# Load order, one more dependence of the planner, and the last stage's sums in two halves: a kernel of a spectral filter and a token MLP

## The chip, the cores and the metric

The kernel runs on one core of a Trainium2 chip. A core has five engines that run side by side and wait for each other by semaphores: TensorE (PE in the profile; its weight loads are PEld) multiplies matrices, VectorE (DVE) and ScalarE (ACT) work element by element, GpSimd (POOL) is nearly unused here, and SyncE (SP) issues the transfers (DMAs). Data lie in SBUF, with 128 partitions; TensorE writes to PSUM, which is handed out in banks. The metric is the device time of one execution in microseconds.

## The reference

Two results are mixed by a gate. Cut to what matters, with x of shape 2048 x 512 (S x D):

```
g = sigmoid((x * gate_w).sum(-1))                    # one number per row of x
a = irfft2(rfft2(x) * (w_r + i w_i))                 # spectral filter, in f32, then bf16
h = layernorm(x)                                      # over D, without weights
u = gelu(einsum("sd,sf->df", h, w1) + b1)            # mixes rows: 2048 -> 1792
b = (einsum("df,fs->ds", u, w2) + b2).T              # 1792 -> 2048
out = g * a + (1 - g) * b
```

Both branches are given the same x, the input A_x; the input B_x is not used. Inputs and output are bf16.

## The kernel before, in words

The 2048 rows are dealt out as 16 blocks j = 4q + r of 128 rows: q is the quarter, r the residue of the row's number modulo 4. A row block is one [128, 512] slice of the tile `x`; the four blocks of one r form a row group.

The work has these stages. (1) Loads of x, group by group, with the transform tables (`ta`, one part per r) and the first-layer weights in between (`w1`, buffer `wa`, first seven column tiles of 128). (2) For each row block VectorE (L487, L488) or ScalarE (L491, L495) takes mean and variance, and ScalarE (L527) or VectorE (L521) writes the normalized h. (3) TensorE multiplies h with w1 (`m1`, L705), seven column tiles side by side in seven PSUM banks, then seven more with the weights in `wb`; ScalarE applies the gelu (L721). (4) Beside it runs the spectral branch: sums over quarters (`q4a`, `q4b`, L535 to L542), a transform over rows on TensorE (`fa`, L554 to L557), copied out by ScalarE (L560), sums (`d2`, L566 and L567), a radix-4 step (`radix4`, L585 to L601), a transform over columns (`fb`, L653, with table `tb`; copied out by L660), sums (`tb2`, L669 to L677), the product with the filter (L820 to L846), and the way back: the inverse radix-4 step, whose two parts of results for each half lt are called ("T", lt, 0) and ("T", lt, 1), the inverse transform over rows (`i1`, L886 to L898, for each r, each half lt and each h) and the sums behind it (L914 to L927). (5) The gate: x times `gate_w` (tile `gw`, L730, VectorE, four times [128, 2048]), summed by ScalarE (L735), then g and 1 - g. This overwrites x, so each multiply has to wait until its group was read by all others. (6) The second layer (`m2`, L1008) for each row block, evacuated by ScalarE with the factor 1 - g (L1014). (7) The last stage, for eight pairs of row blocks p: TensorE transforms over columns (`i3`, L967 to L970), ScalarE copies out with the factor g (L974), VectorE makes the sums of the pair (`es`, L982 to L993: a short copy, an add and a sub into the tile `es`, then an add and a sub out of it), adds the MLP's part (`fin2`, L1027) and SP stores. The last block is finished in parts by L1021.

The order of all this is made by a planner when the kernel is built (class `Plan`, L133). Each task has an engine, a duration, what it reads and writes, a priority (a small number goes first) and, where it uses one of a few buffers, the buffer's name in `alloc` and `free`. The planner simulates all engines with these durations and, whenever an engine is free, takes the ready task of the smallest priority; between tasks of equal priority the one that was added first. A task on the same VectorE is ready only 0.1 us after the task that it depends on ended; in that moment any other ready task is taken. Loads are tasks of SP: nearly all are ready from the start, so SP issues them in the order of their priorities, one at a time, and a load may be issued only when the eighth before it has landed. The resulting order is fixed for each engine; on the chip an engine executes its own list in this order and waits wherever an input is late.

The code names of the loads: `ld([("x", r, q) ...])` x of group r, `ld([("ta", r)])` the row table of group r, `ld_w1` the first weights of group r (for r = 1 in two halves of q), `load_wb(0)` four wide pieces of w1 for `wb`, 512 KB each, `load("gw")` the gate row copied to all partitions, `load("tb")` the column table, `b2h` the second bias, and `ld_W` the complex filter weights.

Of the kernel before, what the change touches and what calls it, by code (L numbers as in the profile page):

```python
# [16 lines left out]
P = 128  # L17
S = 2048
D = 512
# [113 lines left out]
class Plan:  # L133
# [11 lines left out]
    def add(self, eng, dur, emit, reads=(), writes=(), prio=0.0, alloc=(), free=(), nbytes=0, after=(), late=0.0):  # L145
        t = Task()
        t.late = late
        t.eng, t.dur, t.emit, t.prio = eng, dur, emit, prio
        t.alloc, t.free, t.nbytes = tuple(alloc), tuple(free), nbytes
        t.users, t.end, t.ready = [], None, 0.0  # L150
        deps = set(after)
        for k in reads:
            if k in self.last_w:
                deps.add(self.last_w[k])
            self.readers.setdefault(k, []).append(t)
        for k in writes:
            if k in self.last_w:
                deps.add(self.last_w[k])
            deps.update(self.readers.get(k, ()))
            self.last_w[k] = t  # L160
            self.readers[k] = []
        deps.discard(t)
        t.deps = deps
        self.tasks.append(t)
        return t
# [99 lines left out]
def kernel(  # L265
# [22 lines left out]

    pool = ctx.enter_context(tc.tile_pool(name="sb", bufs=1))
    psum = ctx.enter_context(tc.tile_pool(name="ps", bufs=1, space=bass.MemoryType.PSUM))  # L290
    NES = 1

    def sb(shape, dt, tag, bufs=1):
        return pool.tile(shape, dt, tag=tag, name=tag, bufs=bufs)
# [48 lines left out]
    def load(key, shape, dt, src, nbytes, prio=0.0):  # L343
        def emit():
            t[key] = sb(shape, dt, key)
            dma(t[key][:], src)
        return add("SP", 0.5, emit, writes=[key], prio=prio, nbytes=nbytes)

    def ld(keys, dst, src, nbytes, prio, eng="SP"):
        return add(eng, 0.5, lambda: dma(dst(), src, A if eng == "ACT" else None), writes=keys, prio=prio, nbytes=nbytes, after=[a0])  # L350
# [21 lines left out]
    for r in range(4):  # L372
        if r == 0:
            for n, qs in enumerate(XQ):
                ld([("x", 0, q) for q in qs], lambda qs=qs: t["x"][:, qs[0]:qs[-1] + 1:2, 0, :], x4[:, qs[0]:qs[-1] + 1:2, 0, :], 131072 * len(qs), -9 + 0.1 * n)
        else:
            for qs in ((0,), (1,), (2, 3)) if r == 1 else ((0, 1, 2, 3),):
                c = slice(qs[0], qs[-1] + 1)
                ld([("x", r, q) for q in qs], lambda r=r, c=c: t["x"][:, c, r, :], x4[:, c, r, :], 131072 * len(qs), 2 * r - (3 if r == 1 else 0) + 0.01 * qs[0])
        ld([("ta", r)], lambda r=r: t["ta"][:, r, :], tabs["ta"][:, r, :], 163840, 2 * r + (0.6 if r == 1 else 0.2) if r else -0.8)  # L380

    NF = 7
    WB = (0, NF, NF + 4, NFT)
# [23 lines left out]
    def ld_bias():  # L407
        dma(t["b1b"][0:NFT], B_b1.rearrange("(t f) -> t f", f=P))
    add("SP", 0.5, ld_bias, writes=["bias"], prio=7.1, nbytes=4096, after=[a0])
    load("tb", [P, 776], BF16, tabs["tb"], 198656, prio=9)  # L410

    def ld_wb(k, q):
        def emit():
# [10 lines left out]
            add("SP", 0.5, ld_wb(k, q), writes=[("w1", k + 1, 4 * q + r) for r in range(4)], prio=10 + 12 * k + 0.1 * q,  # L424
                nbytes=131072 * (WB[k + 2] - WB[k + 1]), after=after)
    load_wb(0)
    load("gw", [P, D], BF16, gate_w[None, :].to_broadcast([P, D]), 131072, prio=14.5)

    ld(["b2h"], lambda: t["b2h"][:], B_b2.rearrange("(q p r) -> p q r", q=4, r=4), 300000, 14.6)

    wsrc = (A_w_r, A_w_i)

# [440 lines left out]
    for rs, h in ((0, 0), (0, 1), (1, 0), (1, 1)):  # L873
        for r in (rs, rs + 2):
            for lt in range(2):
                tag = ("fa", "fb")[lt]

                def i1(h=h, r=r, lt=lt, tag=tag):
                    if "zz" not in t:
                        t["zz"] = sb([P, 2, 2, 2, 2, 2, 2, P], BF16, "X")  # L880
                        t["ze"] = sb([P, 2, 2, 2, 2, L], BF16, "h")
                    p1 = t["i1", h, r, lt] = ps([P, 2, L], F32, tag, 2)
                    o, w = ti_at(r)
                    ti = t["ti"][:, o:o + w]
                    for v in range(2):
                        d = lambda c: t["B"][:, lt, r, 2 * c + v, h:L:2]  # L886
                        if r % 2:
                            for c in range(2):
                                f = (2 * c if lt == 0 else 5 - c) * P
                                T.matmul(p1[:, v], lhsT=d(c), rhs=ti[:, f:f + L], start=(c == 0), stop=(c == 1))  # L890
                        else:
                            n = 129 if r == 0 and lt == 0 else P
                            u = ti[:, 256 * lt:256 * lt + 256]
                            if n > P:
                                T.matmul(p1[:, v], lhsT=d(1), rhs=t["ti"][:, 2816:3072], start=True, stop=False)
                            else:
                                T.matmul(p1[:, v, n:], lhsT=d(1), rhs=u[:, n:], start=True, stop=True)
                            T.matmul(p1[:, v, 0:n], lhsT=d(0), rhs=u[:, 0:n], start=(n == P), stop=True)  # L898
                i1t[h, r, lt] = add("PE", mm(*([256] * 4 if r % 2 else [128] * 4)), i1, reads=[("T", lt, r % 2), "ti"], writes=[("i1", h, r, lt)], prio=3, alloc=[tag])

                def i1ev(h=h, r=r, lt=lt):
                    if r % 2:
                        o = t["zz"][:, 1, h, lt, :, :, r // 2, :]
                        A.copy(o, t["i1", h, r, lt][:].rearrange("p v (k a) -> p v k a", k=2))
                    else:
                        A.copy(t["ze"][:, h, r // 2, lt], t["i1", h, r, lt][:])
                add("ACT", act(512), i1ev, reads=[("i1", h, r, lt)] + pbk, writes=[("zz" if r % 2 else "ze", h, r, lt)], prio=1.7, free=[tag], after=[lined])

            if r % 2 == 0:
                def zf(h=h, r=r):  # L910
                    e = t["ze"][:, h, r // 2]
                    k0, k1 = (t["zz"][:, 0, h, :, :, k, r // 2, :] for k in range(2))
                    if r == 0:
                        V.tensor_copy(k0[:, :, :, 0], e[:, :, :, 0])  # L914
                        V.tensor_copy(k1[:, :, :, 0], e[:, :, :, P])
                        V.tensor_add(k0[:, :, :, 1:P], e[:, :, :, 1:P], e[:, :, :, P + 1:L])
                        V.tensor_sub(k1[:, :, :, P - 1:0:-1], e[:, :, :, 1:P], e[:, :, :, P + 1:L])
                    else:
                        V.tensor_add(k0, e[:, :, :, 0:P], e[:, :, :, P:L])
                        V.tensor_sub(k1[:, :, :, ::-1], e[:, :, :, 0:P], e[:, :, :, P:L])  # L920
                add("DVE", 2 * tt(512) + (tiny(2) if r == 0 else 0), zf, reads=[("ze", h, r, lt) for lt in range(2)], writes=[("zz", h, r, lt) for lt in range(2)], prio=3.55)

        def fq(rs=rs, h=h):
            z = xph(h)[:, 2048 * rs:2048 * rs + 2048].rearrange("p (q v n) -> p q v n", q=4, v=2)
            a, b = (t["zz"][:, rs, h, i].rearrange("p v k r a -> p k v (r a)") for i in range(2))
            V.tensor_add(z[:, 0:4:3], a, b)
            V.tensor_sub(z[:, 1:3], a[:, ::-1], b[:, ::-1])  # L927
        add("DVE", 2 * tt(1024), fq, reads=[("zz", h, r, lt) for r in (rs, rs + 2) for lt in range(2)] + [("T", 0, 0), ("T", 0, 1), ("T", 1, 0), ("T", 1, 1)],
            writes=[("z", rs, h)] + ([] if rs else ["pp" if h else "xs"]), prio=3.6)
# [27 lines left out]
    for p in range(NJ // 2):  # L957
# [22 lines left out]
            return t["tb_"][:, j0:j0 + 3:2]  # L980

        def es(p=p, j0=j0, late=late, tb2j=tb2j):  # L982
            e, s = eo_v(p), sb([P, 2, 2, 2, P], BF16, "es", NES)
            o = tb2j() if late else e
            if late:
                for i in range(2):
                    V.tensor_scalar_add(e[:, i, 0, 0:129], e[:, i, 0, 0:129], t["ombb2"][:, j0 + 2 * i:j0 + 2 * i + 1])
            o = o.rearrange("p j h (k d) -> p j (h k) d", k=2)
            V.tensor_copy(s[:, :, :, :, 0], e[:, :, :, 0:129:128].rearrange("p j h k -> p j k h"))
            V.tensor_add(s[:, :, 0, :, 1:P], e[:, :, :, 1:P], e[:, :, :, P + 1:L])  # L990
            V.tensor_sub(s[:, :, 1, :, P - 1:0:-1], e[:, :, :, 1:P], e[:, :, :, P + 1:L])
            V.tensor_add(o[:, :, 0:4:3], s[:, :, :, 0], s[:, :, :, 1])
            V.tensor_sub(o[:, :, 2:0:-1], s[:, :, :, 0], s[:, :, :, 1])  # L993
        add("DVE", tiny(1) + 4 * tt(512) + (0.3 if late else 0), es, reads=(k1 + ["omg"]) if late else [],
            writes=ko if late else k1, prio=4, alloc=["es"], free=["es"], after=gates if late else ())

        for i, j in enumerate((j0, j1)):
            n = 2 * p + i
# [77 lines left out]
```

## Time and profile before

| | us |
|---|---|
| median of 3 runs (lowest, highest) | 129.49 (129.37, 129.72) |
| the profiled execution | 129.0 |
| its span, first to last instruction | 127.1 |
| TensorE busy | 122.3 |
| VectorE busy | 114.6 |
| ScalarE busy | 81.3 |

The profile is of one execution. A row of a timeline gives start, duration, engine, line of the kernel, operation, what is written <- what is read with its shape, and how many instructions were merged (x7); in brackets stands how long the engine had been idle and what ended it. A row of the wait view gives who waited <- for whom: total, how many times, the longest. A row of the view by stretches gives the stretch, its length, the busy time of PE, PEld, DVE, ACT and POOL with their numbers of instructions, the granted TensorE clock (1.00 is full), the mean busy share of the 16 DMA engines and GB/s. The line that begins with GB/s gives the rate in 40 equal slices of the span, 3.18 us each. The granted clock was 1.00 over the whole span.

### The profile page before, as it was taken

The page shows a single profiled execution, that of the slowest core. Times are in us where ns is not written, and L with a number is a line of the kernel's source. Part 1 is how long each engine was busy: PE and PEld are TensorE (multiplying, and loading weights), DVE is VectorE, ACT ScalarE, POOL GpSimd, SP SyncE. Part 2 cuts the span into 40 slices and gives each one's busy share as a digit, 9 for nine tenths or more (in the row PEclk, how much of TensorE's full clock was granted, in tenths as well). Part 3 has the DMA queues.
Part 4 walks back from the last instruction along what each step waited for, and adds up shares of the span by engine and source line. Part 5 has one row for each costly group of instructions (what it writes and reads, how often), then busy time and mean ns, then how long its engine had stood idle before and what let it go on. Part 6 is the DMA issues. An engine that isn't in the chain of part 4 may idle for free.

```text
span 127.1 us, 2153 instructions
## 1 busy us (share of the span) xinstructions
PE 122.3 (96%) x756; PEld 68.9 (54%) x756; DVE 114.6 (90%) x273; ACT 81.3 (64%) x165; POOL 0.2 (0%) x4
## 2 busy tenths in 40 slices
PE   6999999999999999999999999999989999999991
PEld 2345555555555466644445555555667767655590
DVE  2789999996999999999999999999989989999951
ACT  0973789699999999999420004722389999952200
POOL 0000000000000000000000000000000000000000
PEclk9999999999999999999999999999999999999999
DMA  2999999995548946899999900000000000006451
GB/s 69 300 355 291 382 366 368 351 325 106 122 107 256 285 96 143 200 406 415 411 409 406 398 29 0 0 5 0 3 0 0 0 5 0 0 0 248 165 211 44
DMA packets 18219, 23.12 MB, mean 182 GB/s; under 512 B 2190, under 2 KB 15904, under 8 KB 18208
## 3 DMA queue, kind: packets, MB, share of 16 engines
q1 hardware_dynamic: 17616, 22.36, 52.8%
q10 hardware_dynamic: 592, 0.62, 1.6%
q8 instruction: 6, 0.10, 0.3%
q14 instruction: 5, 0.04, 0.1%
HBM read 20.86 MB, written 2.10 MB: 181 GB/s over the span
## 4 chain that ended last, share of the span: by engine, by line
DVE 37%; PE 29%; DMA 21%; SPq 8%; issue 2%; DVEq 0%
PE acc L1008 16%; DMA wa<-in_B_w_dram 12%; SPq L306 8%; DMA gw<-in_gate_w_dram 6%; DVE x L730 4%; DVE xp L828 4%; DVE st L828 3%; DMA x<-in_A_x_dram 3%; DVE st L586 3%; PE acc L705 3%; DVE xp L833 2%; DVE xp L585 2%; DVE B L840 2%; DVE xp L834 2%; PE fb L890 1%
## 5 line engine op out<-in xcount | busy, mean ns | idle before, releaser
L705 PE MATMUL acc<-h,wb 128*128 128x512 bf16 x112 | 26.9, 379 | 0.0
L1008 PE MATMUL acc<-gl,wb 128*128 128x512 bf16 (+1 forms) x98 | 24.6, 371 | 0.0
L1008 PE MATMUL acc<-gl,wa 128*128 128x512 bf16 (+1 forms) x98 | 23.8, 371 | 0.0
L1014 ACT ACTIVATE x<-acc,ombb,omg 128x512 bf16<-128x512 f32 x12 | 9.0, 777 | 21.4 <-PE acc L1008 21.4
L1008 PEld LDWEIGHTS <-wa 128*128 128x128 bf16 x126 | 13.5, 113 | 9.9
L1008 PEld LDWEIGHTS <-wb 128*128 128x128 bf16 x126 | 13.3, 113 | 9.3
L705 PE MATMUL acc<-h,wa 128*128 128x512 bf16 x64 | 17.6, 379 | 0.0
L705 PEld LDWEIGHTS <-wb 128*128 128x128 bf16 x112 | 10.7, 98 | 10.5
L705 PEld LDWEIGHTS <-wa 128*128 128x128 bf16 x112 | 10.3, 98 | 10.4 <-issue 0.8
L487 DVE BATCH_NORM_STATS2 stats<-x 128x6 f32<-128x512 bf16 x14 | 9.5, 678 | 1.9 <-DMA x<-in_A_x_dram 1.9
L560 ACT CAST xp<-fa 128x512 bf16<-128x512 f32 x16 | 9.2, 580 | 2.0 <-PE fa L557 2.0
L735 ACT ACTIVATE x<-x 128x512 bf16<-128x512 bf16 x16 | 10.2, 692 | 0.0
L721 ACT ACTIVATE gl<-acc,b1f 128x512 bf16<-128x512 f32 x11 | 7.9, 719 | 3.5 <-PE acc L705 3.5
L705 PE MATMUL fb<-h,wa 128*128 128x512 bf16 x32 | 9.7, 379 | 0.0
L527 ACT ACTIVATE h<-x,nmr,rstd 128x512 bf16<-128x512 bf16 x11 | 8.4, 807 | 1.1 <-DVE nmr L518 1.1
L705 PE MATMUL fa<-h,wa 128*128 128x512 bf16 x16 | 5.9, 381 | 0.1
L653 PEld LDWEIGHTS <-X 128*128 128x128 bf16 x64 | 4.6, 98 | 2.5 <-DVE X L637 0.7
L974 ACT ACTIVATE B<-fa,g 128x512 bf16<-128x512 f32 x8 | 5.6, 704 | 0.2 <-PE fa L970 0.2
L730 DVE TENSOR_TENSOR x<-x,gw 128x2048 bf16<-128x2048 bf16 x4 | 4.8, 1220 | 1.1 <-DMA gw<-in_gate_w_dram 1.1
L974 ACT ACTIVATE B<-fb,g 128x512 bf16<-128x512 f32 x8 | 5.7, 712 | 0.0
L356 PE MATMUL fa<-xp 128*128 128x512 bf16 x10 | 4.4, 632 | 1.2 <-DVE xp L317 1.2
L660 ACT CAST X<-fb 128x512 bf16<-128x512 f32 x8 | 5.1, 636 | 0.0
(169 smaller groups left out, 232.8 us busy)
## 6 DMA issues: line engine op xcount, KB each, us to landing
wb<-in_B_w_dram SPq DMA_DIRECT2D x11, 512.0 KB
wa<-in_B_w_dram SPq DMA_DIRECT2D x7, 512.0 KB
wa<-in_B_w_dram SPq DMA_DIRECT2D x2, 896.0 KB
wb<-in_B_w_dram SPq DMA_DIRECT2D x4, 384.0 KB
out_dram<-x SPq DMA_DIRECT2D x3, 512.0 KB
x<-in_A_x_dram SPq DMA_DIRECT2D x2, 512.0 KB
wa<-in_B_w_dram SPq DMA_DIRECT2D x2, 448.0 KB
rot<-dft_ti SPq DMA_DIRECT2D x1, 768.0 KB
```

The lines of the kernel that those rows point to most:

```text
L306: (eng or nc.sync).dma_start(out=out_ap, in_=in_ap)
L487: V.bn_stats(out=t["stats"][:, j, :], in_=t["x"][:, j // 4, j % 4, :])
L527: add("ACT", 0.71, lambda j=j: A.activation(t["h"][:, j // 4, j % 4, :], t["x"][:, j // 4, j % 4, :], ActF.Identity, bias=t["nmr"][:, j:j ...
L560: add("ACT", act(512), lambda r=r, dq=dq: A.copy(xe(r)[:, :, :, dq, :], t["pa", r, dq][:]), reads=[("pa", r, dq)], writes=[("X", r, dq)], ...
L705: T.matmul(t["u", ft][:], lhsT=w[:, j // 4, j % 4, c * P:(c + 1) * P], rhs=t["h"][:, j // 4, j % 4, :], start=(j == jorder[0]), stop=(j == ...
L721: gelus.append(add("ACT", act(512, 1) , lambda ft=ft: A.activation(t["gl"][:, ft, :], t["u", ft][:], ActF.Gelu_apprx_tanh, bias=t["b1f"][: ...
L730: add("DVE", tt(2048), lambda r=r: V.tensor_mul(t["x"][:, :, r, :], t["x"][:, :, r, :], t["gw"][:, None, :].to_broadcast([P, 4, D])), read ...
L735: A.activation(t["x"][:, q, r, :], t["x"][:, q, r, :], ActF.Copy, accum_out=t["glog"][:, 4 * q + r:4 * q + r + 1])
L828: V.tensor_mul(o, xs, w)
L974: A.activation(eo_v(p)[:, n], t["i3", j][:], ActF.Copy, scale=t["g"][:, j:j + 1])
L1008: T.matmul(t["y", j, m][:, cs], lhsT=w[:, o, 512 * q + r:512 * q + 512:4], rhs=t["gl"][:, ft, cs], start=(ft == 0), stop=(ft == NFT - 1))
L1014: A.activation(tbuf(j).rearrange("p h d -> p (h d)"), t["y", j, 0][:], ActF.Identity, bias=t["ombb2"][:, j:j + 1], scale=t["omg"][:, j:j + 1])
```

## The change

Four things are changed; the instructions that compute are the same, their order is not.

1. The priorities of loads. Issued before, behind the first x and weights: w1 of r = 1 (two halves), ta 1, x 2, ta 2, w1 of r = 2, x 3, ta 3, w1 of r = 3, flip, b1, tb, four wide pieces, gw, b2h. Issued after: w1 of r = 1 (first half), x 2, ta 1, w1 of r = 1 (second half), w1 of r = 2, x 3, ta 2, w1 of r = 3, flip, b1, gw, ta 3, four wide pieces, tb, b2h.
2. In the planner, the inverse transform `i1` of r = 2 is given a dependence on ("T", lt, 1) beside ("T", lt, 0).
3. The sums of the last stage are split into two tasks, `es` (into the tile `es`) and `es2` (out of it). With equal priorities, the planner may take the first half of the next pair between them.
4. The tile `es` has two buffers instead of one.

```diff
-    NES = 1
+    NES = 2
...
-                ld([("x", r, q) for q in qs], lambda r=r, c=c: t["x"][:, c, r, :], x4[:, c, r, :], 131072 * len(qs), 2 * r - (3 if r == 1 else 0) + 0.01 * qs[0])
-        ld([("ta", r)], lambda r=r: t["ta"][:, r, :], tabs["ta"][:, r, :], 163840, 2 * r + (0.6 if r == 1 else 0.2) if r else -0.8)
+                ld([("x", r, q) for q in qs], lambda r=r, c=c: t["x"][:, c, r, :], x4[:, c, r, :], 131072 * len(qs), (0, -0.9 if len(qs) > 1 else -1 + 0.01 * qs[0], 2.503, 4.6)[r])
+        ld([("ta", r)], lambda r=r: t["ta"][:, r, :], tabs["ta"][:, r, :], 163840, (-0.8, 2.505, 6.3, 7.3)[r])
...
-    load("tb", [P, 776], BF16, tabs["tb"], 198656, prio=9)
+    load("tb", [P, 776], BF16, tabs["tb"], 198656, prio=14.7)
...
-    load("gw", [P, D], BF16, gate_w[None, :].to_broadcast([P, D]), 131072, prio=14.5)
+    load("gw", [P, D], BF16, gate_w[None, :].to_broadcast([P, D]), 131072, prio=7.2)
-    ld(["b2h"], lambda: t["b2h"][:], B_b2.rearrange("(q p r) -> p q r", q=4, r=4), 300000, 14.6)
+    ld(["b2h"], lambda: t["b2h"][:], B_b2.rearrange("(q p r) -> p q r", q=4, r=4), 300000, 14.9)
...
-                i1t[h, r, lt] = add("PE", ..., i1, reads=[("T", lt, r % 2), "ti"], ...)
+                i1t[h, r, lt] = add("PE", ..., i1, reads=[("T", lt, r % 2), "ti"] + ([("T", lt, 1)] if r == 2 else []), ...)
...
         def es(p=p, j0=j0, late=late, tb2j=tb2j):
-            e, s = eo_v(p), sb([P, 2, 2, 2, P], BF16, "es", NES)
+            e = eo_v(p)
+            s = t["es", p] = sb([P, 2, 2, 2, P], BF16, "es", NES)
...
             V.tensor_sub(s[:, :, 1, :, P - 1:0:-1], e[:, :, :, 1:P], e[:, :, :, P + 1:L])
+        add("DVE", 0.08 + 2 * tt(512) + (0.45 if late else 0), es, reads=k1 + (["omg"] if late else []), writes=[("es", p)], prio=4, alloc=["es"],
+            after=gates if late else ())
+
+        def es2(p=p, late=late, tb2j=tb2j):
+            s, o = t["es", p], (tb2j() if late else eo_v(p)).rearrange("p j h (k d) -> p j (h k) d", k=2)
             V.tensor_add(o[:, :, 0:4:3], s[:, :, :, 0], s[:, :, :, 1])
             V.tensor_sub(o[:, :, 2:0:-1], s[:, :, :, 0], s[:, :, :, 1])
-        add("DVE", tiny(1) + 4 * tt(512) + (0.3 if late else 0), es, reads=(k1 + ["omg"]) if late else [],
-            writes=ko if late else k1, prio=4, alloc=["es"], free=["es"], after=gates if late else ())
+        add("DVE", 0.01 + 2 * tt(512), es2, reads=[("es", p)] + k1, writes=ko if late else k1, prio=4, free=["es"])
```

More of the change, by code (lines that the diff above doesn't have):

```diff
@@ L898, in i1 @@
                             T.matmul(p1[:, v, 0:n], lhsT=d(0), rhs=u[:, 0:n], start=(n == P), stop=True)
-                i1t[h, r, lt] = add("PE", mm(*([256] * 4 if r % 2 else [128] * 4)), i1, reads=[("T", lt, r % 2), "ti"], writes=[("i1", h, r, lt)], prio=3, alloc=[tag])
+                i1t[h, r, lt] = add("PE", mm(*([256] * 4 if r % 2 else [128] * 4)), i1, reads=[("T", lt, r % 2), "ti"] + ([("T", lt, 1)] if r == 2 else []), writes=[("i1", h, r, lt)], prio=3, alloc=[tag])
                 def i1ev(h=h, r=r, lt=lt):
@@ L982, in es @@
         def es(p=p, j0=j0, late=late, tb2j=tb2j):
-            e, s = eo_v(p), sb([P, 2, 2, 2, P], BF16, "es", NES)
-            o = tb2j() if late else e
+            e = eo_v(p)
+            s = t["es", p] = sb([P, 2, 2, 2, P], BF16, "es", NES)
             if late:
@@ L987, in es @@
                     V.tensor_scalar_add(e[:, i, 0, 0:129], e[:, i, 0, 0:129], t["ombb2"][:, j0 + 2 * i:j0 + 2 * i + 1])
-            o = o.rearrange("p j h (k d) -> p j (h k) d", k=2)
             V.tensor_copy(s[:, :, :, :, 0], e[:, :, :, 0:129:128].rearrange("p j h k -> p j k h"))
```

## The prediction

> **What bounds the kernel now.** I read the page first, then the timeline of TensorE for holes, then who waits for whom, then the chain that ended last, and then the two other engines where a hole of TensorE begins.
>
> ```profile
> span 127.1 us, 2153 instructions
> PE 122.3 (96%) x756; PEld 68.9 (54%) x756; DVE 114.6 (90%) x273; ACT 81.3 (64%) x165; POOL 0.2 (0%) x4
> ```
>
> TensorE (PE) is busy for 96% of the span, VectorE (DVE) for 90%. Ends of matmuls are modelled, so I don't use the busy time but the distance from start to start:
>
> ```profile
> 32.38 0.22 PE L556 MATMUL fa<-rot,gl 128*128 128x128 bf16 x1
> 32.69 0.23 PE L557 MATMUL fa<-rot,gl 128*128 128x128 bf16 x1
> ...
> 39.37 5.56 PE L705 MATMUL acc<-h,wb 128*128 128x512 bf16 x25
> 45.09 0.40 PE L653 MATMUL fa<-tb,X 128*128 128x128 bf16 x4 [0.16 <-DVE X L637]
> ...
> 93.00 0.22 PE L898 MATMUL fb<-rot,B 128*128 128x128 bf16 x1
> 93.61 0.23 PE L897 MATMUL fb<-rot,B 128*128 128x128 bf16 x1 [0.39 <-DVE B L601]
> ...
> 111.96 1.67 PE L1008 MATMUL acc<-gl,wa 128*128 128x512 bf16 x7
> 113.47 1.67 PE L1008 MATMUL acc<-gl,wb 128*128 128x512 bf16 x7
> ```
>
> Seven 512-column matmuls take 113.47 - 111.96 = 1.51 us, 0.216 us each. A 128-column one takes a quarter, about 0.056. With these pitches three real holes stand in the rows: 32.69 - 32.38 - 0.056 = 0.25 us; 45.09 - (39.37 + 25 x 0.216) = 0.33 us; 93.61 - 93.00 - 0.056 = 0.55 us. Together 1.13 us. In the rows of the wait view all three are waits for VectorE:
>
> ```profile
> PEld L557 <- DVE gl L542: 0.2, 1, 0.2
> PEld L653 <- DVE X L637: 0.7, 1, 0.7
> PEld L897 <- DVE B L601: 0.6, 1, 0.6
> DVE x L730 <- DMA gw<-in_gate_w_dram: 1.1, 1, 1.1
> ```
>
> After 93.6 us there is no hole:
>
> ```profile
> 93.60:124.30 30.70, 30.67 (x240) 21.01 (x240) 26.90 (x72) 20.24 (x36) 0.00 (x0) 1.00 0.18 67
> ```
>
> That is length, then busy time of PE, weight loads, DVE, ACT and POOL, the granted clock (1.00) and the DMA columns. TensorE is the bound, its matmuls are not changed by the edit, and time can only come from holes, or be lost by making new ones.
>
> **The change part by part.**
>
> *The gate row (`gw`) ahead of the wide weights.* Before, it is issued after four 512 KB pieces:
>
> ```profile
> 16.36 6.32 SPq L306 DMA_DIRECT2D wb<-in_B_w_dram  x4
> ```
> ```profile
> 23.07 7.65 DMA gw<-in_gate_w_dram
> ```
>
> It lands 7.65 us after its issue, at 30.72, and VectorE's first multiply by it waits:
>
> ```profile
> 25.43 0.39 DVE L566 TENSOR_TENSOR X<-xp 128x512 bf16<-128x512 bf16 x1
> ...
> 30.74 1.23 DVE L730 TENSOR_TENSOR x<-x,gw 128x2048 bf16<-128x2048 bf16 x1 [1.09 <-DMA gw<-in_gate_w_dram]
> 31.88 0.42 DVE L541 TENSOR_TENSOR gl<-st 128x512 bf16<-128x512 bf16 x1
> 32.22 0.42 DVE L542 TENSOR_TENSOR gl<-st 128x512 bf16<-128x512 bf16 x1
> 32.55 2.35 DVE L730 TENSOR_TENSOR x<-x,gw 128x2048 bf16<-128x2048 bf16 x2
> ...
> 44.78 0.25 DVE L637 CAST X<-fx 128x32 bf16<-128x32 f32 x1
> ...
> 52.66 0.69 DVE L669 TENSOR_TENSOR B<-X 128x1024 bf16<-128x1024 bf16 x1
> ...
> 92.87 0.69 DVE L601 TENSOR_TENSOR B<-st 128x1024 bf16<-128x1024 bf16 x1
> ```
>
> After, the row is issued before the four pieces, so it lands before them, by the four issues at least 6.3 us sooner, some 5 us ahead of the multiply. The 1.09 us go. L542 then ends 1.09 earlier (31.5 instead of 32.6), before TensorE asks for it at 32.44: hole 1, 0.25 us, closes. L637 ends at 43.9; TensorE, itself 0.25 earlier, asks at 44.5: hole 2, 0.33, closes too. TensorE is then 0.58 ahead.
>
> What is late next on VectorE is ScalarE (ACT):
>
> ```profile
> 32.96 0.58 ACT L560 CAST xp<-fa 128x512 bf16<-128x512 f32 x1 [0.21 <-PE fa L557]
> 49.03 0.69 ACT L721 ACTIVATE gl<-acc,b1f 128x512 bf16<-128x512 f32 x1 [0.27 <-PE acc L705]
> 51.98 0.65 ACT L660 CAST X<-fb 128x512 bf16<-128x512 f32 x1
> ```
>
> L669 starts at 52.66, 0.03 us after that copy ends (52.63). ScalarE gains only what it waits for TensorE ahead of this, 0.21 + 0.27 = 0.48 us. So of VectorE's 1.09 about 0.5 is left at 52.7, and as no wait of it stands between there and L601, L601 ends at 93.1 instead of 93.6. Bounds for what is left: 0 (if ScalarE is held by something else) and 1.09.
>
> *The wait that the planner now counts.* A row group r = 2 of the inverse transform is now planned after both parts of the sums it reads (`("T", lt, 1)` too), as the chip already makes it wait: the stalled L897 in hole 3 waits for L601. With hole 3 alone unmended TensorE would come to it 0.58 earlier and VectorE 0.5 earlier, and a wait of about 0.6 would stay. With the new dependence the planner puts other matmuls there: the second layer's (L1008), 0.216 us each, three cover 0.65. They are taken from the closed stretch behind, so hole 3, 0.55 us, comes off the end. Cost: the r = 2 products go out up to 0.65 later; what reads them is ScalarE and VectorE in the last stage, whose cover is below. I take 0.55; the ends are 0 (planner finds no filler) and 0.55 + 0.08.
>
> *The other loads.* x of row group 2 goes ahead of half of the r = 1 weights, x of group 3 ahead of two tables, `tb` behind the wide weights, the tables for 2 and 3 later. No statistic but the very first waits for x, and what is moved back has time:
>
> ```profile
> DVE stats L487 <- DMA x<-in_A_x_dram: 1.9, 1, 1.9
> ```
> ```profile
> 16.88 0.38 PE L705 MATMUL fa<-h,wa 128*128 128x512 bf16 x1
> ```
> ```profile
> GB/s 69 300 355 291 382 366 368 351 325 106 122 107 256 285 96 143 200 406 415 411 409 406 398 29 0 0 5 0 3 0 0 0 5 0 0 0 248 165 211 44
> ```
>
> The moved half is behind 3.74 MB in all (itself in it). By the slices of 3.18 us, 0.22 + 0.95 + 1.13 + 0.93 = 3.23 MB are there at 12.7 and the rest at 14.0; if the next piece (0.92 MB) shares the engines, at 16.4. Its first matmul is at 16.88. So 0, with a cover of 0.5 us or more; if that is gone TensorE pays the difference, at most 0.5. `tb` takes the old place of `gw` behind the wide weights, from where a load landed at 30.72, and is read at 45.09; the last table stands ahead of the wide weights, so it lands before that too, and is read at 32.38. The number of DMAs in front of the complex weights is the same, so SP and what queues behind it (their issues, then the second layer's weights) don't move: 0. The small `b1` row keeps its neighbours: 0.
>
> *The last stage in two halves, and the second tile.* Per row pair the same five VectorE instructions; no instruction is added.
>
> ```profile
> 102.67 0.42 DVE L990 TENSOR_TENSOR es<-B 128x508 bf16<-128x508 bf16 x1
> 103.01 0.42 DVE L991 TENSOR_TENSOR es<-B 128x508 bf16<-128x508 bf16 x1
> 103.54 0.43 DVE L992 TENSOR_TENSOR B<-es 128x512 bf16<-128x512 bf16 x1
> ...
> 106.22 0.42 DVE L993 TENSOR_TENSOR B<-es 128x512 bf16<-128x512 bf16 x1
> 106.74 0.19 DVE L989 COPY es<-B 128x8 bf16<-128x8 bf16 x1
> ...
> 120.15 0.68 DVE L1027 TENSOR_TENSOR x<-x,B 128x1024 bf16<-128x1024 bf16 x1
> 121.23 0.75 DVE L1021 SCALAR_TENSOR_TENSOR x<-acc,omg,x 128x512 bf16<-128x512 f32 x1 [0.39 <-PE acc L1008]
> ```
>
> Two sums that don't depend on each other start 0.34 us apart (102.67, 103.01); the second half starts 0.53 after the first: 0.19 lost. A new pair behind the second half starts 0.52 later, 0.18 lost: the one tile is still in use. With the halves alternating and two tiles, eight times the first and three times the second can go: up to 8 x 0.19 + 3 x 0.18 = 2.1 us of VectorE, at least 0. It is off the path: the last sum ends at 120.83 and VectorE then waits 0.39 for TensorE. If TensorE is 1.13 earlier (120.1 instead of 121.23) and VectorE only 0.5 (120.3), VectorE would be 0.2 late for one row block and catch up in the next wait; any third of the 2.1 us covers it. Priced at 0.
>
> *Sum.* 0.25 + 0.33 + 0.55 = 1.13; I take 1.1. The profiled execution took 129.0 for its span of 127.1, so 127.9 after; it is 0.5 below the median of the runs, 129.49, so the median goes to **128.4 us**.
>
> **The rivals.**
>
> *B, only VectorE's half comes through.* The planner finds no useful filler for hole 3, and the wait of 0.6 stays. Then the end moves with L601, by 0.5: 129.0. For it: the planner's times are not the chip's; hole 3 itself shows that. Against: fillers are there in plenty, the L1008 matmuls that now run in closed rows behind 110 us.
>
> *C and D, the multiplies are pulled forward.* With `gw` early, the planner may place the four L730 (1.14 us each from start to start: 30.74 to 31.88) where it sees VectorE free, ahead of the statistics of group 3. Those have no slack:
>
> ```profile
> 27.14 1.52 ACT L527 ACTIVATE h<-x,nmr,rstd 128x512 bf16<-128x512 bf16 x2 [0.23 <-DVE nmr L518]
> ```
> ```profile
> 28.91 0.38 PE L705 MATMUL fa<-h,wa 128*128 128x512 bf16 x1
> ```
>
> ScalarE finishes the last h at 28.66 and TensorE takes it at 28.91, 0.25 later. One multiply ahead costs 1.14 - 0.25 = 0.89 there and leaves the gain of 1.13: about 129.3, no change (C). Two cost 2.28 - 0.25 = 2.03: slower from the second on, 129.49 - 1.13 + 2.03 = 130.4 (D). Against: they have the lowest priority of what VectorE has, and the sums of group 0 (`d2`, L566, which need only ScalarE's copies of that group) were held back for the statistics until 25.43 in the rows above; any free moment of the plan would have gone to them first. That no other small wait of a newly made plan eats the gain is not shown; I count that with C and D.
>
> *E, VectorE is the bound in the last stage.* If TensorE's closed rows are only the model of their ends, VectorE (26.90 of 30.70 busy) sets the end, and the 0.5 and 2.1 us come off: 126.9. Against: the pitch of 0.216 is between starts, not ends, and VectorE waits 0.39 for TensorE before L1021, not the other way.
>
> The Trainium skill ("Perfetto Trace Analysis", section "Identifying the Most-Contended Engine") calls matmul busy time a bad measure and would judge by weight loads, 54% here, so that VectorE with 90% is the engine to relieve: that is rival E, 126.9. Against E speaks another of its pages, "VectorE: DVE Perf Modes", section "The DRAIN you can't avoid": there a semaphore after each of eight chained copies cost nothing, so that splitting the sums would bring VectorE nothing and only 0.5 of E's time is left, 129.0. The rows above disagree with that second rule, 0.53 against 0.34 us.
>
> **How the numbers follow.** Forecast (A, own range 128.1 to 128.8) 0.48, B 0.13, C 0.15, D 0.20, E 0.04. About 0.3%, 0.39 us, is what a measurement of this kernel can tell from no change. A, B and E are faster by more: 0.65; C is within: 0.15; D is slower: 0.20. The range goes from 128.0 (all of 1.13 and the uncertainty of the runs) up to 130.0, over A, B, C and a part of D; E and most of D are left out.
>
> **What would show it.** In the profile after: no wait of L730 for `gw`; L637 done before 44.2; L669 right behind L660, both about 0.5 earlier; no hole of TensorE at L653 and L897, with L1008 rows between the r = 0 and r = 2 products; first halves of two pairs next to each other on VectorE, with starts of L992 0.34 after what is before it; TensorE's last matmul at about 123.2 instead of 124.3. Wrong it is if an L730 stands ahead of a group 3 statistic (L487), if TensorE waits for ScalarE's h (L527) or for the moved weights at 16.9, or if VectorE is later than TensorE at L1021 by more than 0.8.

## The result, and the profile after

The changed kernel takes 127.74 us (median of 5 runs, 127.68 to 128.14) against 129.37 us for the kernel before in the same comparison (5 runs, 128.64 to 129.72). The ratio is 0.990, with a 95% interval from 0.9866 to 0.9933: 1.3 us faster, 0.9 to 1.7 (the two medians lie 1.6 apart). Four of all the executions told of here, three of the kernel before and the profiled one of the split alone (130.87 us, whose trace is therefore not read), took over 1.5% longer than the shortest of their kernel and are left out of every ratio and range. The profiled executions are 129.0 and 127.68 us, their spans 127.1 and 125.9.

The page of the kernel after:

```profile
span 125.9 us, 2138 instructions
PE 120.5 (96%) x743; PEld 68.8 (55%) x756; DVE 113.8 (90%) x273; ACT 81.0 (64%) x165; POOL 0.2 (0%) x4
```

Thirteen records of matmuls are missing in this trace (743 of 756), each of which looks like a hole of 0.2 us in the timeline; they are no waits, and the weight loads are complete. In its wait view there is no wait of L730 for `gw`, and none of TensorE for L542, L637 or L601. VectorE around `gw`, where the code asks for it, and where ScalarE limits it (timeline of the kernel after; L1024 to L1030 are the old L1021 to L1027, L1011 the old L1008):

```profile
25.42 0.39 DVE L566 TENSOR_TENSOR X<-xp 128x512 bf16<-128x512 bf16 x1
...
29.55 1.22 DVE L730 TENSOR_TENSOR x<-x,gw 128x2048 bf16<-128x2048 bf16 x1
30.69 0.42 DVE L541 TENSOR_TENSOR gl<-st 128x512 bf16<-128x512 bf16 x1
31.02 0.42 DVE L542 TENSOR_TENSOR gl<-st 128x512 bf16<-128x512 bf16 x1
31.36 2.36 DVE L730 TENSOR_TENSOR x<-x,gw 128x2048 bf16<-128x2048 bf16 x2
...
43.59 0.25 DVE L637 CAST X<-fx 128x32 bf16<-128x32 f32 x1
47.55 0.69 DVE L669 TENSOR_TENSOR B<-X 128x1024 bf16<-128x1024 bf16 x1 [0.18 <-ACT X L660]
...
52.05 0.69 DVE L669 TENSOR_TENSOR B<-X 128x1024 bf16<-128x1024 bf16 x1
...
92.25 0.69 DVE L601 TENSOR_TENSOR B<-st 128x1024 bf16<-128x1024 bf16 x1
```

The first multiply moves by 1.19 us (30.74 to 29.55), the one L669 after which VectorE follows ScalarE by 0.61 (52.66 to 52.05), and L601 by 0.62 (92.87 to 92.25). A part of what is lost between the first two is seen at 47.55, where VectorE now waits 0.18 for ScalarE.

TensorE at the old hole 3:

```profile
92.39 0.22 PE L898 MATMUL fb<-rot,B 128*128 128x128 bf16 x1
92.44 0.22 PE L897 MATMUL fb<-rot,B 128*128 128x128 bf16 x1
...
92.83 0.22 PE L898 MATMUL fa<-rot,B 128*128 128x128 bf16 x1
93.10 0.60 PE L890 MATMUL fa<-rot,B 128*128 128x256 bf16 x4
93.54 0.22 PE L897 MATMUL fb<-rot,B 128*128 128x128 bf16 x1
```

Before, the `fb` product behind 93.00 stood waiting until L601 was done. Now one with the same form runs at 92.44, while L601 is still at work (92.25 to 92.94), so it can't be the one that needs L601; that one comes later, at 93.54. (One of the missing records belongs between 92.83 and 93.10.) The last group of matmuls starts at 122.55 instead of 123.72, 1.17 us earlier.

The last stage of VectorE:

```profile
104.98 0.42 DVE L989 TENSOR_TENSOR es<-B 128x508 bf16<-128x508 bf16 x1
105.32 0.42 DVE L990 TENSOR_TENSOR es<-B 128x508 bf16<-128x508 bf16 x1
105.65 0.42 DVE L996 TENSOR_TENSOR B<-es 128x512 bf16<-128x512 bf16 x1
105.99 0.42 DVE L997 TENSOR_TENSOR B<-es 128x512 bf16<-128x512 bf16 x1
106.32 0.42 DVE L996 TENSOR_TENSOR B<-es 128x512 bf16<-128x512 bf16 x1
...
117.84 0.69 DVE L1030 TENSOR_TENSOR x<-x,B 128x1024 bf16<-128x1024 bf16 x1
120.05 0.75 DVE L1024 SCALAR_TENSOR_TENSOR x<-acc,omg,x 128x512 bf16<-128x512 f32 x1 [1.52 <-PE acc L1011]
```

In six of the eight pairs the second half of the sums now starts 0.33 us after what stands in front of it, another pair's half, instead of 0.53; the first pair and the last are as before. The last sum ends at 118.53 and VectorE waits 1.52 us for TensorE instead of 0.39.

### The profile page after: what moved, and what is told of

Its sections match the earlier page's. It is cut to its first block, busy times and chain, and to the rows that moved or that the text cites. A ratio compares the mean times of both kernels' runs of the same rounds, so it can differ in the third digit from the quotient of the medians.

```text
span 125.9 us, 2138 instructions
## 1 busy us (share of the span) xinstructions
PE 120.5 (96%) x743; PEld 68.8 (55%) x756; DVE 113.8 (90%) x273; ACT 81.0 (64%) x165; POOL 0.2 (0%) x4
## 4 chain that ended last, share of the span: by engine, by line
PE 73%; DMA 17%; SPq 7%; issue 1%; DVE 0%
PE acc L1011 32%; PE acc L705 20%; DMA wa<-in_B_w_dram 9%; SPq L306 7%; PE fb L1011 5%; DMA wt<-in_A_w_r_dram 5%; DMA x<-in_A_x_dram 3%; PE fb L653 2%; PE fa L653 2%; PE fa L890 2%; PE fb L890 1%; PE fb L705 1%; PE fa L967 1%; PE fb L967 1%; PE fa L1011 1%
## 5 line engine op out<-in xcount | busy, mean ns | idle before, releaser
L705 PE MATMUL acc<-h,wb 128*128 128x512 bf16 x108 | 25.9, 379 | 0.1
L1011 PE MATMUL acc<-gl,wb 128*128 128x512 bf16 (+1 forms) x94 | 23.9, 371 | 0.2
L1011 PE MATMUL acc<-gl,wa 128*128 128x512 bf16 (+1 forms) x97 | 23.8, 371 | 0.1
L1011 PEld LDWEIGHTS <-wa 128*128 128x128 bf16 x126 | 13.5, 113 | 9.9
L1011 PEld LDWEIGHTS <-wb 128*128 128x128 bf16 x126 | 13.3, 113 | 9.3
L653 PEld LDWEIGHTS <-X 128*128 128x128 bf16 x64 | 4.7, 98 | 2.1
L660 ACT CAST X<-fb 128x512 bf16<-128x512 f32 x8 | 5.1, 634 | 0.0
L660 ACT CAST X<-fa 128x512 bf16<-128x512 f32 x8 | 5.0, 620 | 0.0
L356 PE MATMUL fa<-xp 128*128 128x512 bf16 x10 | 3.8, 549 | 1.2 <-DVE xp L317 1.2
```

Source lines behind the costliest of these rows:

```text
L653: T.matmul(pb[:, k % 2, k // 2], lhsT=t["X"][:, lt, EX[e], c, k, :], rhs=tbl(k, c), start=True, stop=True)
L660: A.copy(t["X"][:, lt, EX[e]].rearrange("p c j l -> p (c j l)").rearrange("p (h c g b) -> p h c g b", h=2, c=2, b=2)[:, :, c], t["pb", lt, ...
L705: T.matmul(t["u", ft][:], lhsT=w[:, j // 4, j % 4, c * P:(c + 1) * P], rhs=t["h"][:, j // 4, j % 4, :], start=(j == jorder[0]), stop=(j == ...
L1011: T.matmul(t["y", j, m][:, cs], lhsT=w[:, o, 512 * q + r:512 * q + 512:4], rhs=t["gl"][:, ft, cs], start=(ft == 0), stop=(ft == NFT - 1))
```

## The experiments

My theory (T): TensorE's matmuls run without a gap except in three holes (and three smaller ones ahead of 17 us, 0.22 to 0.28, 0.19 and 0.14, which the change leaves), and a part of the change is worth the holes that it closes: the early gate row holes 1 and 2 (0.58 us), the dependence hole 3 (0.55), the split and the other loads nothing. The main rivals: VectorE sets the end in the last stage, so that the split pays (E), and the three holes are one, so that one of the two parts is enough (B2). A hole is counted as in the prediction, from start to start. All ratios are to the kernel before on the same chip.

**The gate row alone.**

```diff
-    load("gw", ..., 131072, prio=14.5)
+    load("gw", ..., 131072, prio=7.2)
```

> Only the gate row's priority is changed (14.5 to 7.2); the lists of TensorE, VectorE and ScalarE stay as before, only the list of SP differs. Theory T (TensorE's closed rows set the end, a part is worth the holes it closes): the wait of L730 for gw goes, holes 1 and 2 close (0.25 + 0.33 us), hole 3 stays at about 0.55 because VectorE's L601 and TensorE both come some 0.6 earlier: 0.6 us faster. Rival B2 (the three holes are one: once VectorE is earlier, hole 3 closes too): 1.1 to 1.2 faster. Rival N (ScalarE passes nothing on): hole 3 grows and 0.0 to 0.1 is left.

Ratio 0.9908 (0.9874 to 0.9942). The profiled execution took 128.33 us, 0.7 less than that of before. TensorE at hole 3:

```profile
92.39 0.22 PE L898 MATMUL fb<-rot,B 128*128 128x128 bf16 x1
92.99 0.23 PE L897 MATMUL fb<-rot,B 128*128 128x128 bf16 x1 [0.38 <-DVE B L601]
...
123.11 0.55 PE L1008 MATMUL fb<-gl,wb 128*128 128x128 bf16 x7
```

Hole 3 is there with 92.99 - 92.39 - 0.056 = 0.54, the other two are gone, and the last group starts 0.61 earlier (123.11). That is T in the trace, and speaks against B2 and N. The ratio does not fit it: about 1.2 us, with an interval that leaves T's 0.6 out and has B2's value in it. Against B2 stand the hole in this trace, the span of e3 (125.9 against 126.5 here) and e8; what the ratio has beyond the trace is taken up at the end.

**The dependence alone.**

```diff
-    reads=[("T", lt, r % 2), "ti"]
+    reads=[("T", lt, r % 2), "ti"] + ([("T", lt, 1)] if r == 2 else [])
```

> Only the dependence of i1 for r = 2 on both parts of T is added. Theory T: holes 1 and 2 stay as before, hole 3 closes, 0.5 to 0.6 us faster. Rival B2 (the dependence does nothing by itself): 0. Rival of a delayed last stage: hole 3 closes and VectorE is late at the end, 0 or slower.

Ratio 0.9970 (0.9941 to 0.9999), 0.4 us; the profiled execution took 128.53.

```profile
30.97 1.23 DVE L730 TENSOR_TENSOR x<-x,gw 128x2048 bf16<-128x2048 bf16 x1 [0.87 <-DMA gw<-in_gate_w_dram]
```
```profile
39.60 5.56 PE L705 MATMUL acc<-h,wb 128*128 128x512 bf16 x25
45.32 0.40 PE L653 MATMUL fa<-tb,X 128*128 128x128 bf16 x4 [0.16 <-DVE X L637]
...
93.12 0.22 PE L898 MATMUL fb<-rot,B 128*128 128x128 bf16 x1
...
93.23 0.22 PE L898 MATMUL fb<-rot,B 128*128 128x128 bf16 x1
93.29 0.22 PE L897 MATMUL fb<-rot,B 128*128 128x128 bf16 x1
...
93.73 0.38 PE L1008 MATMUL acc<-gl,wb 128*128 128x512 bf16 x1
```

The wait for `gw` is nearly as before, hole 2 is as before (0.32), hole 3 is closed. Hole 1 is gone too, against the expectation: TensorE comes to that place 0.46 later, for a reason told at the end, and hardly waits there. In the lists of the engines the order of forms on TensorE is the same as before; only VectorE's sums behind it changed places: L914 to L917, which need r = 0, now come for both values of h ahead of L919 and L920, which need r = 2. So the filler is not a second-layer matmul: two products of `i1` with the same shape have changed places, r = 0 of the second h and r = 2 of the first.

**Gate row and dependence together** (both edits above).

> The gate row early and the dependence of i1; no other load moved, sums of the last stage not split, one es tile. Theory T: all three holes close, 1.1 to 1.2 us faster, the same as the whole change within 0.2. Rival E (VectorE sets the end in the last stage): at most 0.6 of it, the rest needs the split.

Ratio 0.9879 (0.9836 to 0.9922). The span is 125.9, that of the whole change, and the last group of matmuls starts at 122.56. E falls here: without the split the whole of the shorter span is there. VectorE reaches the last block with nothing to spare:

```profile
119.30 0.69 DVE L1027 TENSOR_TENSOR x<-x,B 128x1024 bf16<-128x1024 bf16 x1
120.06 0.75 DVE L1021 SCALAR_TENSOR_TENSOR x<-acc,omg,x 128x512 bf16<-128x512 f32 x1
121.58 0.48 DVE L1021 SCALAR_TENSOR_TENSOR x<-acc,omg,x 128x256 bf16<-128x256 f32 x1 [0.78 <-PE acc L1008]
```

L1021 has no wait in front of it, and starts at the same 120.06 as with the whole change (120.05).

**The whole change again, on the same chip.**

> The whole change once more, for comparison on the same chip: 1.1 to 1.5 us faster by every theory.

Ratio 0.9859 (0.9812 to 0.9906), its four runs 127.68 to 127.70; that of gate row and dependence alone, 0.9879, lies within its interval. What the split and the other loads add is not more than these intervals can tell. But all four runs of the whole change lie below all six of gate row and dependence alone (127.77 to 128.14), so 0.1 to 0.2 us more is not excluded. The traces do not show where it would come from: both spans are 125.9 and the last group starts at 122.56 and 122.54.

**The last stage alone.**

```diff
-    NES = 1
+    NES = 2
...
-    es (whole)
+    es (into the tile), es2 (out of it)
```

(The last two lines in words; the code stands in the diff of the change.)

> Only the last stage: sums in two halves and two es tiles. Theory T: VectorE gets 1.5 to 2.1 us shorter there and waits that much longer for TensorE before the last block's sums; the three holes stay; time the same within 0.3%. Rival E (VectorE sets the end): 1.5 to 2.1 us faster.

Ratio 1.0012 (0.9981 to 1.0042): nothing, and E's 1.5 to 2.1 us (1.2 to 1.6%) are excluded.

The Trainium skill ("Perfetto Trace Analysis", section "Identifying the Most-Contended Engine") names two measures instead of matmul busy time, the share of the peak rate that the matmuls reach (MFU) and the busy share of weight loads. The prediction used the second alone, 54% here against VectorE's 90%. These runs disagree with what follows from that one: in the whole change VectorE's wait in front of the last block is 1.1 us longer (1.52 against 0.39), and the split alone does not move the end. The first was not worked out here. Its page "VectorE: DVE Perf Modes", section "The DRAIN you can't avoid", says that semaphores between chained copies cost nothing. Here a dependent sum that follows directly starts 0.45 to 0.53 us after the one before it (0.52 or 0.53 in six of the eight pairs before) and 0.33 with other work in between, so for these the trace disagrees.

**The other loads alone**, with the gate row's priority as before.

```diff
+    x 2: 2.503, ta 1: 2.505, x 3: 4.6, ta 2: 6.3, ta 3: 7.3, tb: 14.7, b2h: 14.9   (gw stays at 14.5)
```

(In words; the code stands in the diff of the change.)

> Only the other loads (x of groups 2 and 3 earlier, two tables later, tb and b2h later), the gate row late as before; lists of all engines but SP as before. Theory T: 0, the three holes stay. Rival L (the earlier x is worth something, or a later weight or table costs): 0.2 to 0.5 either way.

Ratio 0.9968 (0.9944 to 0.9992), 0.4 us faster: this expectation was wrong. I had overlooked that `tb`, moved from 9 to 14.7, goes behind `gw` even where that stays at 14.5 (no run moves `tb` by itself); the row is issued 1 us sooner (22.02 instead of 23.07), and in the profiled execution it came in time:

```profile
22.02 0.71 SPq L306 DMA_DIRECT2D gw<-in_gate_w_dram  x1
22.78 0.43 SPq L306 DMA_DIRECT2D tb<-dft_tb  x1
```
```profile
29.56 1.22 DVE L730 TENSOR_TENSOR x<-x,gw 128x2048 bf16<-128x2048 bf16 x1
```

With no wait there the trace is that of the gate row alone: hole 3 with 0.55, last group at 123.12. So in this trace what these loads are worth goes by way of `gw`, and there is nothing beyond it. It is the shortest of the 12 runs, though (128.39; median 128.83): in the others the row may have come late again, which no trace shows.

**The whole change with the gate row late, and without the dependence.**

```diff
-    load("gw", ..., 131072, prio=7.2)
+    load("gw", ..., 131072, prio=14.5)
```

> The whole change but the gate row, which goes back behind the wide weights. Theory T: VectorE waits about 1 us for gw again, holes 1 and 2 are back (0.58), hole 3 stays closed: 0.5 to 0.6 us faster than before. Rival B2: 0.

Ratio 0.9917 (0.9892 to 0.9943), 1.1 us, more than expected. Again `gw` stands ahead of `tb`: in the profiled execution L730 waits 0.61 instead of 1.09, hole 1 doesn't come back (TensorE itself is 0.32 later there), hole 2 is 0.14, hole 3 is closed.

```profile
30.59 1.23 DVE L730 TENSOR_TENSOR x<-x,gw 128x2048 bf16<-128x2048 bf16 x1 [0.61 <-DMA gw<-in_gate_w_dram]
```

```diff
-    reads=[("T", lt, r % 2), "ti"] + ([("T", lt, 1)] if r == 2 else [])
+    reads=[("T", lt, r % 2), "ti"]
```

> The whole change without the dependence of i1. Theory T: hole 3 is back with about 0.55, holes 1 and 2 stay closed: 0.6 us faster than before. Rival B2: 1.1 to 1.2 faster, the dependence is worth nothing once VectorE is earlier.

Ratio 0.9947 (0.9919 to 0.9975), 0.7 us. In its trace hole 3 is back with 0.55 (93.24 behind 92.63), the other two stay closed. That is T, against B2.

**What the split is good for.** The same 2.2 us of added work on VectorE, whose result is not used, ahead of the last pair, once in the whole change and once in gate row and dependence alone, which has no split:

```diff
             if late:
+                V.tensor_add(t["st"][:], t["st"][:], t["st"][:])
```

> The whole change, with one idle piece of work put on VectorE ahead of the last pair's first half: an add of st to itself, 128 x 4096, about 2.2 us, whose result nobody reads. Theory T (the split is worth 1.5 us of cover in front of L1024 and nothing else): the wait of 1.52 us takes most of it, the rest the waits behind it; time as the whole change, within 0.2 us. Rival E (VectorE sets the end): 2.2 us slower than the whole change.

> Gate row and dependence alone (sums not split), with the same 2.2 us on VectorE ahead of the last pair. There VectorE reached L1021 with no wait at all (120.06). Theory T: L1021 starts at about 122.3, its four parts follow one another without waits, the last ends at about 124.0 instead of 123.5: 0.4 to 0.6 us slower than without the added work. Rival E: 2.2 us slower. If the split gave no cover, e9 would be as late as this one.

With the split the ratio is 0.9896 (0.9856 to 0.9936), span 125.9: the added work costs nothing. Without, 0.9967 (0.9942 to 0.9991), span 127.0: 1.1 us longer than without the added work (0.9879 and 125.9, in e3), about twice the expected 0.4 to 0.6. First VectorE with the split, then without:

```profile
120.49 0.75 DVE L1025 SCALAR_TENSOR_TENSOR x<-acc,omg,x 128x512 bf16<-128x512 f32 x1
121.58 0.48 DVE L1025 SCALAR_TENSOR_TENSOR x<-acc,omg,x 128x256 bf16<-128x256 f32 x1 [0.34 <-PE acc L1012]
```
```profile
121.68 0.68 DVE L1028 TENSOR_TENSOR x<-x,B 128x1024 bf16<-128x1024 bf16 x1
122.28 1.14 DVE L1022 SCALAR_TENSOR_TENSOR x<-acc,omg,x 128x512 bf16<-128x512 f32 x2
...
123.59 0.34 DVE L1022 SCALAR_TENSOR_TENSOR x<-fb,omg,x 128x128 bf16<-128x128 f32 x1
```

VectorE ends only 0.43 later than without the added work (123.93 against 123.50), as expected; 0.16 of that was there ahead of the added work, since in this execution TensorE waited for `b1` at 23.84 (L1028 of the pair before starts at 116.86 against 116.70). The other 0.7 us are behind VectorE's end. L1028, which ends a pair of quarter 2, comes at 121.68, and the store of 512 KB that waits for it now moves with the last small stores. GB/s from 120 to 128 us in 40 slices of 0.2 us, without added work (e3) and with it (e10):

```profile
GB/s 82 0 0 0 328 451 369 389 348 451 277 343 277 15 79 259 21 13 149 3 0 3 155 6 0 41 0 0 0 0 0 0 0 0 0 0 0 0 0 0
```
```profile
GB/s 82 0 0 0 0 0 0 0 0 0 0 0 0 0 0 0 451 369 430 348 471 369 277 338 307 267 210 139 0 0 0 0 0 0 0 0 0 0 0 0
```

In the first the block of 277 to 451 GB/s is over at 122.6, in the second it runs from 123.2 to 125.6, small stores included. That this store holds up the last ones is read from this one pair of traces; no run moves it alone. So the split is a cover (time by which VectorE may be late before the end moves), of 1.5 us on VectorE and with it for a store, and worth nothing until it is used.

**A try at the first hole that is left**, at 7.34 us (0.28 us), with the thought that weights are late there:

```diff
-    ld([("x", 0, q) for q in qs], ..., -9 + 0.1 * n)
+    ld([("x", 0, q) for q in qs], ..., (-9, -3.95)[n])
```

> The whole change, and the load of x, row group 0, quarter 3, issued behind the first weights of quarter 1 (priority -9 + 0.1 to -3.95), so that the weights of quarter 2 have less beside them. Theory T: TensorE's hole at 7.34 us (0.28) closes or halves, 0.1 to 0.3 us faster than the whole change, if the statistic of that block does not come late for it. Rival: the hole is not the weights' but h's, or the fourth block's statistic is late: 0 to 0.7 slower.

Ratio 0.9893 (0.9858 to 0.9929), as the whole change. The hole is where it was, TensorE's last two rows around it unchanged to 0.01 us:

```profile
6.63 0.59 PE L705 MATMUL fb<-h,wa 128*128 128x512 bf16 x2
7.34 0.38 PE L705 MATMUL fa<-h,wa 128*128 128x512 bf16 x1
```

That speaks against the weights and for the rival, h of the second block. VectorE's row in the whole change points the same way:

```profile
6.88 0.41 DVE L521 TENSOR_SCALAR h<-x,mv,rstd 128x512 bf16<-128x512 bf16 x1
```

It ends at 7.29 (7.28 in e11), and the matmul starts at 7.34 in both. No run moves that h.

## Why the prediction was right, point by point

*Bound and sum.* Right. The forecast was 0.25 + 0.33 + 0.55 = 1.13 us by closed holes; the last group of TensorE moves by 1.17, and the tail behind it is unchanged. Profiled execution against profiled execution it is 1.3 (129.0 to 127.68), of which 1.17 are that. The median of 127.74 lies 0.3 below the stated range, and 0.7 below the point of 128.4; the ratio of 0.990, put on the median of 129.49 that the forecast started from, gives 128.2 (127.8 to 128.6). The mis-sized term is the start, not a hole: I took the profiled execution of before as typical and moved the median by the same 1.1. It is one of the better ones. That the first ratio came so near to the sum is in part luck: on the chip of e1 to e4 the same kernel gained 1.8 us (1.2 to 2.4), more than the closed holes, and what the rest is stays open.

*The wait for `gw`.* Right that it goes and that holes 1 and 2 go with it (e1, e8). What the step did not see is that this wait is not a fixed 1.09 us. With the row behind the wide weights L730 waited 1.09 and 0.87 us with the loads in the old order (before, e2), and 0.61 and 0 with the row one place earlier (e7, e6); I sized it by one of them. In e2 the row lands even later than before (30.95 against 30.72); the wait is shorter because VectorE comes 0.46 later (its L536 at 29.42 against 28.96).

*ScalarE is late next.* Right in kind; sized too small. I gave ScalarE 0.21 + 0.27 = 0.48 and VectorE 0.5. L660 went from 51.98 to 51.38, 0.60, and L669 and L601 follow with 0.61 and 0.62. The wait at 49.03 is for TensorE, and ScalarE follows that through: TensorE is 0.61 earlier at its first L653 (45.09 to 44.48).

*The counted wait.* Right in its worth, 0.55, alone and together with the gate row (e2, e8, e3), so rival B, that it finds no filler, is out. The filler was wrong: I put three second-layer matmuls there, the planner put in two products of the same inverse transform, for which nothing has to be taken from later. The forecast sum is the same either way, because every filler is work that is due anyhow.

*The other loads.* The price of 0 holds in the trace for what I priced: statistics, first weights, tables. Missed was that moving `tb` behind `gw` is by itself a move of `gw` (e6).

*The split.* Right: priced at 0 on the path (e5: 1.0012). Of the up to 2.1 us on VectorE 1.46 came: its last sum ends at 118.53 against 119.99 in e3. I expected VectorE 0.2 us late without it; it is 0.0 late (e3). A cover was right in kind: without the split e10 has none.

*C and D.* Out: the multiplies stand where they stood, behind the last L536; in the traces the order of TensorE's, VectorE's and ScalarE's instructions has no difference ahead of the inverse transform.

*E.* Out by e3, e5 and e9: its 126.9 needed the split to pay by itself.

## What to carry to other kernels

Where one engine is busy almost all the time, count its few gaps from start to start, price each part of a change by the gap that it closes, and price at zero whatever only makes another engine shorter; then say how late that engine may now be before the end moves. A small load that somebody needs early doesn't belong behind large ones: its wait is not a constant, and a single profiled execution gives one value of it (here 1.09 and 0.87 us in one order of the loads, 0.61 and 0 with the row one place earlier). When a planner's dependence is weaker than what the chip really waits for, the fix costs no instruction: tell the planner, and here it found other work.

## What had not been expected

Executions of the kernel before vary more than those with the gate row early. On the chip of e1 to e4 the kernel before ran in 128.62 to 130.21 us (17 runs) and e2, with the late row, in 127.87 to 129.63 (12 runs); e1 in 128.24 to 128.38 (7), e3 in 127.77 to 128.14 (6), the whole change in 127.68 to 127.70 (4). A varying landing of `gw` can make a part of that, since with the loads in one order it came at 30.72 and at 30.95. It is not all: e1 gains 0.6 us by its trace, 0.9 by the medians and 1.2 by its ratio, and among e5 to e8, on the same chip later, the run with an early row and no dependence (e8) varies from 128.26 to 129.12 as well. In its trace and in e2's and e7's the first seven matmuls lose 0.2 to 0.5 us more than in the others, ahead of all that the change touches.

The rows show how. At first TensorE's 512-column matmuls start 0.43 us apart, twice the later 0.216, and when this ends differs from trace to trace. The whole change, then e2 (L356 are ten matmuls at the start whose result is not used):

```profile
1.21 3.77 PE L356 MATMUL fa<-xp 128*128 128x512 bf16 x10 [1.21 <-DVE xp L317]
...
5.77 1.02 PE L705 MATMUL acc<-h,wa 128*128 128x512 bf16 x4
```
```profile
1.21 4.45 PE L356 MATMUL fa<-xp 128*128 128x512 bf16 x10 [1.21 <-DVE xp L317]
...
5.93 1.60 PE L705 MATMUL acc<-h,wa 128*128 128x512 bf16 x4
```

The same four matmuls take 1.02 and 1.60 us. The profile gives the granted clock as 1.00 over both stretches, so that figure does not show it. By the second row block this makes e2, e7 and e8 0.46, 0.32 and 0.22 us later than the trace of the kernel before. With that their traces fit T: e2 closes 0.55 + 0.23 and loses 0.46, and its last group starts 0.33 earlier; e7 and e8 come to 0.67 and 0.36 by the same count and have 0.69 and 0.37. Whether the end of the slow pace goes with the order of the loads was not tried and stays open, and so does how much of the spread of the unprofiled runs it makes.

The second surprise is the 0.7 us behind VectorE's end in e10: the last stores are done later when the 512 KB store of another quarter is still on its way, so that the moment of a large store has its own cover. One pair of traces shows it.
